# Merged batch rests, 512-token blocks, and float32 loads on SP's queue in a retention + feed-forward kernel

## The chip, the cores and the metric

The kernel runs on one core of a Trainium2 chip. The metric is the device time of one execution in microseconds (us); the median of three runs of the kernel before is 343.9 (343.79 to 344.42). The core has TensorE (PE in the profile; its weight loads are PEld), VectorE (DVE), ScalarE (ACT), GpSimd (POOL) and SyncE (SP). Here POOL and SP also issue DMA transfers: POOL those that change the type on the way, SP the others and the DMA transposes. SBUF is the working memory, PSUM the memory that TensorE writes its results to.

## The reference

Retention (attention without softmax, with a decay per head), then a feed-forward layer with hardswish:

```python
# q, k, v: (8 batches, 8 heads, 576 tokens, 64) float32
scores = scale * q @ k.T                      # scale = 1/8
gamma  = 1 - 2 ** (-5 - head)
ret    = scores * gamma ** (i - j)  where i >= j, else 0
x      = (ret @ v), heads side by side        # (4608, 512)
h      = x @ w_in                             # w_in  512 x 2048
g      = h * clip(h + 3, 0, 6) / 6
out    = g @ w_out                            # w_out 2048 x 512, out (4608, 512) float32
```

## The kernel before

**Retention, by chunks.** Each batch of 576 tokens is cut into four chunks of 128 tokens and a rest of 64, 40 chunks in all. The decay inside a chunk is split into factors: Q is multiplied by `gqk` (or `gqv[0]`), V by `gqv[1]`, so that only a 0/1 mask is left between them. What earlier chunks of the batch give to a chunk goes through a state, `ts`, which is kept in two block-diagonal tiles `tbd`, so that one matmul does two heads. A chunk takes these steps:

- load of q, k and v (L75): three transfers on POOL, float32 in DRAM to float16 in SBUF, runs of 64 elements;
- the transposes of Q and K to `qk`: chunks 0 to 5 by TensorE (L157, then VectorE L159/L163 or ScalarE L161), the others by DMA transposes on SP (L177), where Q is first scaled by VectorE together with V (`vs`, L181);
- `scores`: eight matmuls to PSUM `sc` (L192), then VectorE's multiplication with the mask to `at` (L196);
- `inter`: four matmuls of the state with Q (L208; left out in the first chunk of a batch);
- `intra_and_update`: eight matmuls of `at` with V, added to the same PSUM tile `o` (L218); eight matmuls for the update `u` (L227, not in the last chunk of a batch); ScalarE's copy of `o` to `xt16` (L230); VectorE's `ta` and `ts` (L234 to L238); ScalarE's two copies to `tbd` (L241, L242).

**Feed-forward, by blocks.** The 4608 rows of `xt16` are taken in nine blocks of 512, in the order of the tokens. A block spans chunks of two batches, as 512 does not divide by 576. `g1` (L258) makes one of 16 column groups of the hidden layer: four matmuls (L265) to a PSUM tile `ph`, of which there are three, ScalarE's relu to `u` (L269), VectorE's min and product to `gt` (L271). `g2` (L276) makes a quarter of the sum of one of the block's four output tiles: four matmuls (L283); after the fourth quarter ScalarE copies the tile (L287) and SP stores it (L289).

**The order** is written by hand: every engine works in the order of the program text. POOL issues chunks 0 to 3, the four parts of `win`, chunks 4 and 5, the four parts of `wout`, chunks 6 to 8 (L312 to L322), and later a chunk seven ahead of the one that is transposed (L372). Chunks 0 to 3 are done first; then g1 of block 0 begins with chunks 4 and 5 put between its units; then 192 columns of block 1. From there `run` (L387) puts the pieces of retention evenly between units of g1 of the next block and g2 of this one. `do_piece` (L369) is half a chunk's work: in its first half it issues chunk c's DMA transposes, in its second half it does `inter` of c−2, `scores` of c−1 and `intra_and_update` of c−2. VectorE's `at` and `vs` of the first chunks are put off by `later` until the unit after (`run_later`, L141).

Of the kernel before, what the change touches and what calls it, by code (L numbers as in the profile page):

```python
# [18 lines left out]
def kernel(  # L19
# [26 lines left out]
    NMB = NTOK // MBLK  # L46

    chunks = []
    for b in range(B):
        for s0 in range(0, S, P):  # L50
            chunks.append((b, s0, min(P, S - s0)))
    NCHK = len(chunks)
    lng = [float(np.log(1.0 - 2.0 ** (-5.0 - h))) for h in range(H)]

    const = ctx.enter_context(tc.tile_pool(name="const", bufs=1))
    big = ctx.enter_context(tc.tile_pool(name="big", bufs=1))
    nat = ctx.enter_context(tc.tile_pool(name="nat", bufs=10))
# [8 lines left out]
    loaded = {}  # L66

    def load_part(c, which):
        b, s0, n = chunks[c]
        if which == 0:  # L70
            loaded[c] = (nat.tile([P, 2, H, D], FP16, tag="qv", name=f"qv_{c}"),
                         nat.tile([P, H, D], FP16, tag="kn", name=f"kn_{c}"))
        qv, kn = loaded[c]
        t, src = ((qv[:, 0], q), (kn, k), (qv[:, 1], v))[which]
        nc.gpsimd.dma_start(t[0:n], src[b, :, s0:s0 + n, :].rearrange("h s d -> s h d"))  # L75

    def load_chunk(c):
        for which in range(3):
            load_part(c, which)

    def load_win(f0, f1):
        nc.gpsimd.dma_start(
            win16[:, :, f0:f1],
            moe_w_in.rearrange("(cc p) f -> p cc f", p=P)[:, :, f0:f1])

    def load_wout(c0, c1):
        nc.gpsimd.dma_start(
            wout16[:, c0:c1, :],
            moe_w_out.rearrange("(cc p) n -> p cc n", p=P)[:, c0:c1, :])


    load_part(0, 0)
# [8 lines left out]
    load_part(0, 1)  # L101
# [4 lines left out]
    load_part(0, 2)  # L106
# [14 lines left out]
    gc = const.tile([P, NPAIR], FP32)  # L121
    nc.scalar.activation(gc, lgc, ACTF.Exp, scale=float(P))
# [6 lines left out]
    for i in range(2):  # L129
        t = const.tile([P, NPAIR, P], FP16, name=f"tbd{i}")  # L130
        nc.vector.memset(t, 0.0)
        tbd.append(t)

    mask_b = mask01[:, None, :].to_broadcast([P, H, P])
    gc_b = gc[:, :, None].to_broadcast([P, NPAIR, D])


    st = {}
    later = []

# [4 lines left out]

    def transposes(c, apart=False):

        b, s0, n = chunks[c]
        qv, kn = loaded[c]
# [3 lines left out]
        ps = psum.tile([P, 2, NPAIR, P], FP16, tag="tu", name=f"tr_{c}")  # L153
        pk = psum.tile([P, NPAIR, P], FP16, tag="ph", bufs=3, name=f"trk_{c}") if apart else ps[:, 1]
        for dst, src in ((ps[:, 0], qv[:, 0]), (pk, kn)):
            for p in range(NPAIR):
                nc.tensor.transpose(dst[:, p, 0:n], src[0:n, 2 * p:2 * p + 2, :], ident16[0:n, 0:n])  # L157
        if apart:
            nc.vector.tensor_tensor(out=qk[:, 0, :, 0:n], in0=ps[:, 0, :, 0:n],  # L159
                                    in1=gqk[:, 0, :, 0:n], op=ALU.mult)  # L160
            nc.scalar.copy(qk[:, 1, :, 0:n], pk[:, :, 0:n])  # L161
        else:
            nc.vector.tensor_tensor(out=qk[:, :, :, 0:n], in0=ps[:, :, :, 0:n],  # L163
                                    in1=gqk[:, :, :, 0:n], op=ALU.mult)
        later.append(lambda: nc.vector.tensor_tensor(
            out=vs[0:n, 1], in0=qv[0:n, 1], in1=gqv[0:n, 1], op=ALU.mult))

    def transposes_by_dma(c):

        b, s0, n = chunks[c]  # L170
        qv, kn = loaded[c]
# [4 lines left out]
        def transpose(which, src):  # L176
            nc.sync.dma_start_transpose(qk[:, which, :, 0:n],  # L177
                                        src[0:n].rearrange("s h d -> s (h d)"))

        transpose(1, kn)  # L180
        nc.vector.tensor_tensor(out=vs[0:n], in0=qv[0:n], in1=gqv[0:n], op=ALU.mult)  # L181
        transpose(0, vs[:, 0])

    def scores(c):
        b, s0, n = chunks[c]
# [3 lines left out]
        for p in range(NPAIR):  # L189
            for h2 in range(2):  # L190
                r = slice(h2 * HALF, h2 * HALF + HALF)
                nc.tensor.matmul(sc[0:n, h2, p, 0:n], qk[r, 1, p, 0:n], qk[r, 0, p, 0:n],  # L192
                                 start=True, stop=True)
# [3 lines left out]
            out=at[0:n].rearrange("t a b s -> t (a b) s")[:, :, 0:n],  # L197
            in0=sc[0:n].rearrange("t a b s -> t (a b) s")[:, :, 0:n],
            in1=mask_b[0:n, :, 0:n], op=ALU.mult))

    def inter(c):
        b, s0, n = chunks[c]
        o = psum.tile([P, NPAIR, P], FP32, tag="o", name=f"o_{c}")
        st[c]["o"] = o
        if s0 == 0:
            return
        for p in range(NPAIR):
            nc.tensor.matmul(o[:, p, 0:n], tbd[c % 2][:, p, :], st[c]["qk"][:, 0, p, 0:n],  # L208
                             start=(p == 0), stop=False, skip_group_check=True)

    def intra_and_update(c):
        b, s0, n = chunks[c]
        qv, kn = loaded[c]
        o, at, vs = st[c]["o"], st[c]["at"], st[c]["vs"]
        for p in range(NPAIR):
            for h2 in range(2):
                r = slice(h2 * HALF, h2 * HALF + HALF)
                nc.tensor.matmul(o[r, p, 0:n], vs[0:n, 2 * p + h2, :], at[0:n, h2, p, 0:n],  # L218
                                 start=(s0 == 0 and p == 0), stop=(p == NPAIR - 1),
                                 skip_group_check=True)  # L220
        last = s0 + n == S
        if not last:
            u = psum.tile([P, NPAIR, D], FP32, tag="tu", name=f"u_{c}")
            for p in range(NPAIR):
                for h2 in range(2):
                    r = slice(h2 * HALF, h2 * HALF + HALF)
                    nc.tensor.matmul(u[r, p, :], kn[0:n, 2 * p + h2, :], vs[0:n, 2 * p + h2, :],  # L227
                                     start=(p == 0), stop=(p == NPAIR - 1), skip_group_check=True)
        g0 = b * S + s0
        nc.scalar.copy(xt16[:, :, g0:g0 + n], o[:, :, 0:n])  # L230
        if not last:
            ts = work.tile([P, NPAIR, D], FP16, tag="ts", bufs=2, name=f"ts_{c}")
            if s0 == 0:
                nc.vector.tensor_tensor(out=ts, in0=u, in1=gc_b, op=ALU.mult)  # L234
            else:
                ta = work.tile([P, NPAIR, D], FP32, tag="ta", bufs=2, name=f"ta_{c}")
                nc.vector.tensor_tensor(out=ta, in0=u, in1=st[c - 1]["ts"], op=ALU.add)  # L237
                nc.vector.tensor_tensor(out=ts, in0=ta, in1=gc_b, op=ALU.mult)  # L238
            st[c]["ts"] = ts
            nxt = tbd[(c + 1) % 2]  # L240
            nc.scalar.copy(nxt[0:HALF, :, 0:D], ts[0:HALF])  # L241
            nc.scalar.copy(nxt[HALF:P, :, D:2 * D], ts[HALF:P])  # L242
# [3 lines left out]
    def step(c, end=False):  # L246

        if c > 0:
            inter(c - 1)
        if not end:  # L250
            scores(c)
        if c > 0:
            intra_and_update(c - 1)


    gts = {}

    def g1(kb, fc, a, b_):  # L258
# [4 lines left out]
        ph = psum.tile([P, MBLK], FP32, tag="ph", bufs=3, name=f"ph_{kb}_{fc}_{a}")  # L263
        for dmc in range(NCC):
            nc.tensor.matmul(ph[:, 0:b_ - a], win16[:, dmc, P * fc:P * fc + P],  # L265
                             xt16[:, dmc, t0 + a:t0 + b_],
                             start=(dmc == 0), stop=(dmc == NCC - 1))
        u = work.tile([P, MBLK], FP32, tag="moeu", bufs=3, name=f"u_{kb}_{fc}_{a}")
        nc.scalar.activation(u[:, 0:b_ - a], ph[:, 0:b_ - a], ACTF.Relu,  # L269
                             bias=cb[:, 0:1], scale=1.0 / 6.0)  # L270
        nc.vector.scalar_tensor_tensor(out=gt[:, fc, a:b_], in0=u[:, 0:b_ - a], scalar=1.0,  # L271
                                       in1=ph[:, 0:b_ - a], op0=ALU.min, op1=ALU.mult)
# [3 lines left out]
    def g2(kb, mc, part, tag="pout"):  # L276
# [8 lines left out]
        if part == 3:  # L285
            osb = work.tile([P, DM], FP32, tag="osb", bufs=4, name=f"osb_{kb}_{mc}")
            nc.scalar.copy(osb, pout)  # L287
            r0 = kb * MBLK + P * mc
            nc.sync.dma_start(out[r0:r0 + P, :], osb)  # L289

    def g2_halves(kb, mc):
        gt = gts[kb]
        r0 = kb * MBLK + P * mc
        W = DM // 2
        for half in range(2):
# [7 lines left out]
            nc.sync.dma_start(out[r0:r0 + P, half * W:half * W + W], osb)  # L303


    def chunk_of(tok):
        b, s = divmod(tok, S)
        return b * ((S + P - 1) // P) + s // P

    WQ = DFF // 4  # L310
    NEAR = 9
    for c in range(1, 4):  # L312
        load_chunk(c)
    for i in range(4):
        load_win(i * WQ, i * WQ + WQ)
    for c in range(4, 6):
        load_chunk(c)
    for i in range(4):
        load_wout(4 * i, 4 * i + 4)
    for c in range(6, NEAR):  # L320
        load_chunk(c)
    next_load = [NEAR]  # L322


    transposes(0, apart=True)
    run_later(9)
    scores(0)
    run_later(9)
    for c in range(1, 4):
        transposes(c, apart=True)  # L330
        run_later(9)
        step(c)
        run_later(9)
    step(4, end=True)

    def unit1(kb, lo, hi, a=0, b_=MBLK):
        for fc in range(lo, hi):
            g1(kb, fc, a, b_)
            run_later(1)

    def start_of(c):
        b, s0, n = chunks[c]
        return b * S + s0


    unit1(0, 0, 9)
    make_gq()
    transposes(4)
    unit1(0, 9, 10)
    scores(4)  # L350
# [101 lines left out]
```

## Time and profile before

| what | value |
|---|---|
| median of 3 runs | 343.9 us |
| span of the profiled execution | 342.7 us |
| PE busy | 306.4 us (89%), 2304 matmuls |
| VectorE / ScalarE / GpSimd busy | 188.1 (55%) / 176.8 (52%) / 108.0 (32%) |
| loads issued by POOL (L75), q, k and v | 120, 0.86 to 0.88 us each at the mean |
| 512-column matmuls of g1 and g2 (mean) | 384 and 383 ns, overlapped |
| DMA packets on POOL's queue / on SP's | 116,736 / 38,736 |
| HBM read / written | 36.70 / 9.44 MB |

The profile is of one execution. A group line gives the line of the program, the engine, the operation, the output and its inputs, shapes and count, then the busy time, the mean duration, and the idle time ahead of it with what ended it. Timeline lines give the start and the length (from the first start to the last end when several instructions are merged, xcount), and in brackets the idle time before. Matmuls are pipelined, so their lengths overlap, and prices are better taken from start to start. The table of stages gives the busy time per engine in a stretch of the span.

### The profile page before, as it was taken

How to read it: one execution, taken by the hardware profiler on the slowest of the kernel's cores; microseconds unless marked ns; L12 is line 12 of the kernel's file. 1: busy time of each engine (PE TensorE's matmuls, PEld its weight loads, DVE VectorE, ACT ScalarE, POOL GpSimd, SP SyncE). 2: the span in 40 equal slices, each digit the busy share in tenths (PEclk: the TensorE clock that was granted, in tenths of full speed). 3: DMA queues.
4: the chain of work that ended last, by engine and by line, in shares of the span. 5: the costliest groups of instructions: out<-in, count | busy, mean ns of one | idle time of the engine just before them, and what ended most of it. 6: DMA issues, size and time to landing. Idle time of an engine off the chain costs nothing.

```text
span 342.7 us, 5990 instructions
## 1 busy us (share of the span) xinstructions
PE 306.4 (89%) x2304; PEld 158.1 (46%) x2304; DVE 188.1 (55%) x316; ACT 176.8 (52%) x327; POOL 108.0 (32%) x137
## 2 busy tenths in 40 slices
PE   2669767549989999999999999999999999999995
PEld 1443344225654454444455445444444444444444
DVE  2565675244676665666665766655576565443400
ACT  6346574034755565545555656545665556544411
POOL 8947389582338034603442344100000000000000
PEclk9999999896999999999999999999999999999999
DMA  9999999999699999977999499522133221000022
GB/s 62 148 202 183 193 141 150 159 154 175 84 123 149 125 100 145 146 94 90 111 129 133 81 135 142 83 70 63 48 78 76 65 71 37 31 33 31 31 80 76
DMA packets 155502, 36.19 MB, mean 106 GB/s; under 512 B 146641, under 2 KB 150993, under 8 KB 155473
## 3 DMA queue, kind: packets, MB, share of 16 engines
q0 software_dynamic: 116736, 18.36, 79.9%
q1 hardware_dynamic: 38736, 17.44, 23.5%
q8 instruction: 18, 0.29, 0.4%
q14 instruction: 12, 0.09, 0.1%
HBM read 36.70 MB, written 9.44 MB: 135 GB/s over the span
## 4 chain that ended last, share of the span: by engine, by line
PE 82%; DMA 5%; ACT 5%; DVE 3%; issue 2%; POOL 1%; SPq 0%; POOLq 0%; DVEq 0%; ACTq 0%
PE ph L265 36%; PE pout L283 34%; PE o L218 4%; DMA qk<-vs 4%; PE sc L192 4%; PE o L208 2%; ACT xt L230 2%; DVE gt L271 2%; ACT u L269 1%; DMA qv<-in_v_dram 1%; PE pout L298 1%; PE u L227 1%; DVE at L196 1%; POOL qv L75 1%; POOL kn L75 0%
## 5 line engine op out<-in xcount | busy, mean ns | idle before, releaser
L271 DVE SCALAR_TENSOR_TENSOR gt<-u,ph 128x512 f16<-128x512 f32 (+2 forms) x160 | 99.8, 631 | 91.8 <-ACT u L269 90.0
L265 PE MATMUL ph<-xt,win 128*128 128x512 f16 (+2 forms) x640 | 141.8, 365 | 6.5 <-ACT xt L230 4.8
L269 ACT ACTIVATE u<-ph,cb 128x512 f32<-128x512 f32 (+2 forms) x160 | 100.6, 644 | 67.2 <-PE ph L265 64.7
L283 PE MATMUL pout<-wout,gt 128*128 128x512 f16 x560 | 134.3, 383 | 0.0
L265 PEld LDWEIGHTS <-win 128*128 128x128 f16 x640 | 60.9, 99 | 68.7 <-issue 10.7
L283 PEld LDWEIGHTS <-gt 128*128 128x128 f16 x560 | 54.3, 98 | 63.8 <-issue 1.3
L75 POOL DMA_DIRECT2D kn<-in_k_dram x40 | 34.2, 856 | 98.8 <-PE u L227 80.9
L196 DVE TENSOR_TENSOR at<-sc,mask 128x1024 f16<-128x1024 f32 (+1 forms) x40 | 44.4, 1110 | 6.2 <-PE sc L192 6.2
L230 ACT CAST xt<-o 128x512 f16<-128x512 f32 (+1 forms) x40 | 21.7, 543 | 37.2 <-PE o L218 36.6
L287 ACT COPY osb<-pout 128x512 f32<-128x512 f32 x35 | 20.5, 585 | 35.6 <-PE pout L283 35.5
L75 POOL DMA_DIRECT2D qv<-in_q_dram x40 | 35.1, 877 | 3.1 <-DMA wout<-in_moe_w_out_dram 1.7
L75 POOL DMA_DIRECT2D qv<-in_v_dram x40 | 34.5, 862 | 4.0 <-DMA wout<-in_moe_w_out_dram 1.7
L192 PE MATMUL sc<-qk 64*128 64x128 f16 (+1 forms) x320 | 16.4, 226 | 13.0 <-DMA qk<-vs 9.2
L237 DVE TENSOR_TENSOR ta<-u,ts 128x256 f32<-128x256 f32 x24 | 10.1, 423 | 24.8 <-PE u L227 24.8
L181 DVE TENSOR_TENSOR vs<-qv,gqv 128x1024 f16<-128x1024 f16 (+1 forms) x34 | 23.0, 681 | 0.0
L241 ACT COPY tbd<-ts 64x256 f16<-64x256 f16 x32 | 12.9, 404 | 13.6 <-DVE ts L238 12.9
L192 PEld LDWEIGHTS <-qk 64*128 64x128 f16 (+1 forms) x320 | 9.7, 102 | 20.3 <-issue 13.1
L218 PE MATMUL o<-at,vs 128*64 128x128 f16 (+1 forms) x320 | 16.9, 231 | 1.8 <-DVE at L196 1.8
L208 PE MATMUL o<-qk,tbd 128*128 128x128 f16 (+1 forms) x128 | 12.4, 224 | 3.1 <-ACT tbd L242 3.1
L208 PEld LDWEIGHTS <-tbd 128*128 128x128 f16 x128 | 9.6, 103 | 11.3 <-ACT tbd L242 4.5
L218 PEld LDWEIGHTS <-vs 128*64 128x64 f16 (+1 forms) x320 | 10.4, 115 | 6.2 <-DVE at L196 2.3
L242 ACT COPY tbd<-ts 64x256 f16<-64x256 f16 x32 | 12.8, 401 | 0.4
(39 smaller groups left out, 72.7 us busy)
## 6 DMA issues: line engine op xcount, KB each, us to landing
out_dram<-osb SPq DMA_DIRECT2D x35, 256.0 KB, 2.4
qv<-in_q_dram POOLq DMA_DIRECT2D x32, 128.0 KB, 5.0
kn<-in_k_dram POOLq DMA_DIRECT2D x32, 128.0 KB, 4.5
qv<-in_v_dram POOLq DMA_DIRECT2D x32, 128.0 KB, 5.0
win<-in_moe_w_in_dram POOLq DMA_DIRECT2D x4, 512.0 KB, 10.4
wout<-in_moe_w_out_dram POOLq DMA_DIRECT2D x4, 512.0 KB, 9.5
qk<-kn SPq DMA_TRANSPOSE x34, 3.5
qk<-vs SPq DMA_TRANSPOSE x34, 2.6
```

Of the source, the lines that this page charges most:

```text
L75: nc.gpsimd.dma_start(t[0:n], src[b, :, s0:s0 + n, :].rearrange("h s d -> s h d"))
L181: nc.vector.tensor_tensor(out=vs[0:n], in0=qv[0:n], in1=gqv[0:n], op=ALU.mult)
L192: nc.tensor.matmul(sc[0:n, h2, p, 0:n], qk[r, 1, p, 0:n], qk[r, 0, p, 0:n], start=True, stop=True)
L196: later.append(lambda: nc.vector.tensor_tensor(out=at[0:n].rearrange("t a b s -> t (a b) s")[:, :, 0:n], in0=sc[0:n].rearrange("t a b s -> ...
L208: nc.tensor.matmul(o[:, p, 0:n], tbd[c % 2][:, p, :], st[c]["qk"][:, 0, p, 0:n], start=(p == 0), stop=False, skip_group_check=True)
L218: nc.tensor.matmul(o[r, p, 0:n], vs[0:n, 2 * p + h2, :], at[0:n, h2, p, 0:n], start=(s0 == 0 and p == 0), stop=(p == NPAIR - 1), skip_grou ...
L230: nc.scalar.copy(xt16[:, :, g0:g0 + n], o[:, :, 0:n])
L265: nc.tensor.matmul(ph[:, 0:b_ - a], win16[:, dmc, P * fc:P * fc + P], xt16[:, dmc, t0 + a:t0 + b_], start=(dmc == 0), stop=(dmc == NCC - 1))
L269: nc.scalar.activation(u[:, 0:b_ - a], ph[:, 0:b_ - a], ACTF.Relu, bias=cb[:, 0:1], scale=1.0 / 6.0)
L271: nc.vector.scalar_tensor_tensor(out=gt[:, fc, a:b_], in0=u[:, 0:b_ - a], scalar=1.0, in1=ph[:, 0:b_ - a], op0=ALU.min, op1=ALU.mult)
L283: nc.tensor.matmul(pout, gt[:, fc, P * mc:P * mc + P], wout16[:, fc, :], start=(fc == 0), stop=(fc == NFC - 1))
L287: nc.scalar.copy(osb, pout)
```

## The change

- **Pieces instead of chunks.** Each batch gives four pieces of 128 tokens. The rests of two batches are one piece of 128 rows: pieces 12, 21, 30 and 35 of 36. Such a piece has a block-diagonal mask, takes `inter` from two states, and makes no update. There are five `tbd` tiles that are handed out in turn. For odd batches the last state is scaled by the decay of 64 instead of 128 tokens.
- **Blocks of one batch.** `xt16` is ordered so that block kb, up to 7, is the first 512 tokens of batch kb, and block 8 holds all rests. The stores go to the matching rows; those of block 8 are two transfers of 64 rows each.
- **Loads.** Q and V are loaded as float32 by SP (`load_f32`), for the rests as two halves. VectorE casts V, and Q where it goes to a DMA transpose, in `vs`. For pieces 0 to 7 a GpSimd copy makes a float16 Q (`q16`). K of pieces 0 to 3 is loaded as float32 by SP too and cast by GpSimd; all other K stay on POOL as before. The float32 loads of pieces 4 to 7 wait for parts of win and wout to land. Later loads are issued four pieces ahead.
- **Start.** The transposes of pieces 0 to 7 are done by TensorE (before: chunks 0 to 5). In pieces 0 to 3, `update_mm` comes right after `scores`, and K is transposed before Q, each in its own PSUM tile.
- **Block 1** is done in four strips of 128 columns, each when its piece is ready; a `ph` tile then holds four column groups, so 16 matmuls of 128 columns take the place of four of 512.

The core of the diff:

```diff
-        t, src = ((qv[:, 0], q), (kn, k), (qv[:, 1], v))[which]
-        nc.gpsimd.dma_start(t[0:n], src[b, :, s0:s0 + n, :].rearrange("h s d -> s h d"))
+    def load_f32(dst, src, c, behind=None):
+        for p0, b, s0, n in pieces[c][3]:
+            dma = nc.sync.dma_start(dst[p0:p0 + n],
+                                    src[b, :, s0:s0 + n, :].rearrange("h s d -> s h d"))
...
+    def load_qv(c, behind=None):
+        qv = nat.tile([P, 2, H, D], FP32, tag="qv", bufs=6, name=f"qv_{c}")
+        loaded[c]["qv"] = qv
+        load_f32(qv[:, 0], q, c, behind)
+        load_f32(qv[:, 1], v, c)
...
+    def cast_early(c):
+        nc.gpsimd.tensor_copy(loaded[c]["kn"], loaded[c]["k32"])
+        q16 = nat.tile([P, H, D], FP16, tag="q16", bufs=3, name=f"q16_{c}")
+        loaded[c]["q16"] = q16
+        nc.gpsimd.tensor_copy(q16, loaded[c]["qv"][:, 0])
...
+        if kind == "main":
+            states = [(state_of[b], slice(0, P))]
+        else:
+            states = [(state_of[2 * b], slice(0, HALF)), (state_of[2 * b + 1], slice(HALF, P))]
+        for j, (state, cols) in enumerate(states):
+            for p in range(NPAIR):
+                nc.tensor.matmul(o[:, p, cols], tbd[state][:, p, :], qk[:, 0, p, cols],
+                                 start=(j == 0 and p == 0), stop=False, skip_group_check=True)
...
+        n = b_ - a
+        nf = MBLK // n
+        ph = psum.tile([P, nf, n], FP32, tag="ph", bufs=3, name=f"ph_{kb}_{f0}_{a}")
+        for j in range(nf):
+            for dmc in range(NCC):
+                fc = f0 + j
+                nc.tensor.matmul(ph[:, j, :], win16[:, dmc, P * fc:P * fc + P],
...
+    for c in range(EARLY):
+        cast_early(c)
+    wi = [load_win(i * WQ, i * WQ + WQ) for i in range(4)]
+    for c in (4, 5):
+        load_k16(c)
+        load_qv(c, behind=wi[c - 3])
+    wo = [load_wout(4 * i, 4 * i + 4) for i in range(4)]
+    for c in (6, 7):
+        load_k16(c)
+        load_qv(c, behind=wo[c - 4])
...
+    for c in range(EARLY):
+        transposes(c, apart=True)
+        run_later(9)
+        if c > 0:
+            inter(c - 1)
+            intra(c - 1)
+            update_state(c - 1)
+        scores(c)
+        update_mm(c)
+        run_later(9)
...
     def do_piece():
         c, half = divmod(done[0], 2)
         c += FIRST
-        while next_load[0] < NCHK and next_load[0] <= c + 7:
-            load_chunk(next_load[0])
-            next_load[0] += 1
+        load_until(c + 4)
...
+    run([unit1(0, f) for f in range(13)])
+    make_gq()
+    make_mask_rest()
+    first_half(4)
+    run([unit1(0, 13), unit1(0, 14)])
+    scores(4)
+    run([unit1(0, 15)])
+    first_half(5)
+    second_half(4)
+    scores(5)
+    run([unit1(1, f, 0, P) for f in (0, 4)])
+    second_half(5)
+    run([unit1(1, f, 0, P) for f in (8, 12)])
+    run([unit1(1, f, P, 2 * P) for f in range(0, NFC, 4)])
...
+    run([unit1(1, f, 2 * P, 3 * P) for f in range(0, NFC, 4)])
+    load_until(8)
+    first_half(7)
+    run([unit2(0, 3, 1)])
+    scores(7)
+    run([unit2(0, 3, 2)])
+    second_half(7)
+    run([unit2(0, 3, 3)])
+    gts.pop(0)
+    run([unit1(1, f, 3 * P, 4 * P) for f in range(0, NFC, 4)], 3)
+
+    run([unit2(1, mc, part) for mc in range(2) for part in range(4)], pieces_for(2))
```

`first_half(c)` is the GpSimd cast of Q and TensorE's transposes, `second_half(c)` is `inter`, `intra` and the update. From piece 8 on `do_piece` does what it did. The first `do_piece` falls into the last strip of block 1; its `load_until` issues pieces 9 to 12, and stands in SP's order behind the store of output tile (0, 3).

## The prediction

> **What bounds the kernel now.** I read the busy table, then the stages, then the chain of waits and the timelines inside the first two stages. The stage table (length, busy time of each engine, clock, DMA share, GB/s):
>
> ```profile
> core 0: us, PE busy (x) PEld busy (x) DVE busy (x) ACT busy (x) POOL busy (x), PEclk, DMA share, GB/s
> 0.00:24.36 24.36, 11.68 (x140) 8.44 (x141) 11.81 (x32) 11.66 (x28) 19.38 (x31) 1.00 1.44 133
> 24.36:78.55 54.19, 38.49 (x312) 20.70 (x312) 28.96 (x54) 25.22 (x55) 37.04 (x46) 0.95 2.14 167
> 78.55:339.30 260.75, 256.26 (x1852) 128.99 (x1851) 147.37 (x232) 139.67 (x244) 51.59 (x62) 0.99 0.78 91
> ```
>
> Three stages: **head** (0 to 24.36, until the first matmul of g1), **early** (to 78.55, where PE is idle 15.7 us) and **late** (PE busy 98%). Late can be shortened by less PE work only, head and early by removing waits. The early waits are seen in PE's timeline; the bracket is the idle time and what ended it:
>
> ```profile
> 62.96 0.61 PE L192 MATMUL sc<-qk 64*128 64x128 f16 x8 [4.75 <-DMA qk<-vs]
> ...
> 76.88 0.42 PE L192 MATMUL sc<-qk 64*64 64x64 f16 x8 [3.52 <-DMA qk<-vs]
> ```
>
> So TensorE waits for DMA transposes of chunks 6 to 9, in a time in which POOL issues loads back to back. Unit prices come from start-to-start distances in the same timeline, where PE is never idle:
>
> ```profile
> 37.34 0.39 PE L157 MATMUL tr<-ident,qv 128*128 128x128 f16 x4
> 37.57 0.39 PE L157 MATMUL tr<-ident,kn 128*128 128x128 f16 x4
> 37.79 1.03 PE L265 MATMUL ph<-xt,win 128*128 128x512 f16 x4
> ...
> 126.82 0.39 PE L208 MATMUL o<-qk,tbd 128*128 128x128 f16 x4
> 127.14 0.40 PE L192 MATMUL sc<-qk 64*128 64x128 f16 x8
> 127.47 0.41 PE L218 MATMUL o<-at,vs 128*64 128x128 f16 x8
> 127.71 0.29 PE L227 MATMUL u<-vs,kn 128*64 128x64 f16 x8
> 127.94 1.90 PE L283 MATMUL pout<-wout,gt 128*128 128x512 f16 x8
> ```
>
> Four 128-column matmuls take 0.23 us (transposes) to 0.32 us (inter). A full chunk costs 0.32 + 0.33 + 0.24 + 0.23 = 1.12 us. Eight 512-column matmuls take 1.73 us in the chain of waits, so g1 or g2 of a block is 64 of them, 13.84 us. A half chunk costs 0.69 us (0.21 at 84.75, 0.24 at 108.00, 0.24 at 85.29).
>
> **Late stage.** Of its 264.15 us to the end of the span I count 252.9 as PE work: columns 192 to 511 of block 1 in g1 (8 matmuls per 1.10 us at 85.53: 8.8), half of g2(0) (6.9), seven g1 (96.9), eight g2 (110.7), the chunks 9 to 39 (24 × 1.12 − 6 × 0.32 for the first of a batch + 7 × 0.69 − 0.24 done before = 29.6). The other 11.2 us are the tail (3.4), the wait for xt at each block (0.55) and small waits. After the change this stage begins with g1(2): half of g2(1) 6.9, seven g1 96.9, seven g2 96.9, and pieces 12 to 35: twenty full ones (22.4 − 5 × 0.32) and four merged rests. A merged rest costs 8 × 0.0525 (inter, 64 columns) + 0.33 + 0.24 = 0.99 us against 2 × 0.69; scores of piece 12 come earlier. Sum 24.4, total 225.1. I keep the 11.2 us of waits and add 0.5, since the last block's rows go out in two stores each (an SP issue of 0.33 and a little): **236.8 us**.
>
> VectorE's vs now reads float32. The nearest rows are the f16 one of before and the one with a float32 input from PSUM of the same size:
>
> ```profile
> L196 DVE TENSOR_TENSOR at<-sc,mask 128x1024 f16<-128x1024 f32 x32 | 39.0, 1218 | 6.2 <-PE sc L192 6.2
> L181 DVE TENSOR_TENSOR vs<-qv,gqv 128x1024 f16<-128x1024 f16 x27 | 18.3, 683 | 0.0
> ```
>
> I take the first, 1.22 us, so 28 × 0.54 = 15 us more on VectorE. It is 57% busy in the late stage and becomes about 62%, so I cost that at nothing there; its cover is ph's three buffers. If it is gone, each of 24 pieces costs up to 0.54 us, 13 us. Loads now run four pieces ahead instead of seven; at about 7 us a piece that is 28 us, against a median of 5.0 from issue to landing, so nothing is charged for it.
>
> **Head.** Before, `at` of chunks 0 to 3 starts at 8.57, 13.53, 17.59 and 21.50, and g1 2.86 us after the last. After, SP starts the loads at about 1.2 us with no constants between them, but two GpSimd casts per piece are new. No cast is in the trace: iota of 64 and 128 elements took 0.20 and 0.26, which extends to 0.61 us for 512; affine_select of 128 took 0.30, four times that is 1.2. I take 0.8, nearer the lower row, since both only write or copy. The first load landed 3.46 us after its issue (4.78 − 1.32); a 256 KB store on SP took 2.4. Between, the first K is there at about 4.1, the first cast Q near 6, the first `at` near 8.0. Then VectorE sets the pace in the new order: qk 0.42, vs 0.68, ta 0.42, ts 0.42, at 1.22 = 3.17, with gaps 3.25 us per piece against 4.3 on average before. The last `at` starts at 17.75, and 2.65 later (tbd is ready sooner) g1 starts: **20.4 us**; bounds 19.5 (casts 0.61) and 24.4 (nothing gained). Loads hold this while three take under 3.25 us. The win loads now queue behind the casts on POOL, about 14.5 instead of 13.12, but behind fewer open loads; they landed 2.5 us apart before, so the first lands near 20. A late one costs its delay one to one. Three more memsets of tbd (0.27 each) and one more exp (0.19) lie in the first 4 us, where both engines wait for loads; uncovered they cost 1.0.
>
> **Early.** Work from the first g1 to g1(2): g1(0) 13.84; g1 of block 1 in four strips, 16 groups of 16 matmuls at 4 × 0.23, 14.7 (20.5 by the inter row; I take the transposes, which like these run many in a row); g2(0) 13.84; half of g2(1) 6.92; pieces 4 to 7 with transposes 4 × 1.58 − 0.32 = 6.0; pieces 8 to 11 and the scores of 12, 4.5. Sum 59.8. Waits that stay: the slow start of the clock (36 matmuls took 10.05 instead of 7.8) 2.3; `at` and qk of pieces 4 and 5, as now 1.3 + 1.8 and some, 4.3; pieces 6 and 7, 1.
>
> The new wait is on **SP**. In the program's order the loads of pieces 9 to 12 stand behind the store of (0, 3), and the DMA transposes of piece 8 behind these ten loads. The issue time of a float32 load of 1,024 runs on SP, I, is not in the trace. The rows (SPq, start, duration):
>
> ```profile
> 60.96 0.64 SPq L289 DMA_DIRECT2D out_dram<-osb  x1
> 61.71 1.29 SPq L177 DMA_TRANSPOSE qk<-kn  x1
> ...
> 73.55 0.33 SPq L289 DMA_DIRECT2D out_dram<-osb  x1
> ```
>
> Bounds: 0.33 (a store alone) and 1.29 (a transpose); POOL took 0.87 for the same 1,024 runs. I take **0.6**, the row of the same kind of instruction on the same queue with another in front. From the end of g2(0) on PE: store issued 1.85 us later; six loads and four halves at 0.75 I, 9 I; two transposes 2.5; landing 1.4 after the last issue; then four more pieces, each 2 I + 2.5, one store 0.5, and 1.1 from the scores of piece 12 to g1(2). That is 17.35 + 17 I = **27.5 us**, in which PE has 3.7 + 6.9 + 4.5 = 15.1 of work: 12.4 of wait, the place of the 15.7 now. Early: 59.8 + 2.3 + 4.3 + 1 + 12.4 = **79.8**.
>
> **Sum.** 20.4 + 79.8 + 236.8 = 337.0 us of span. The median of the runs, 343.9, stands 1.2 over the profiled span of 342.7; with that **338.2 us**, −1.7%. About 4 of the 5.7 us are the head's; the strips and rests give the rest.
>
> The Trainium skill, "DMA: Bandwidth & Descriptors", section Issuing engines are not separate DMA queues, says that loads issued from another engine run on the same DMA engines and save only issue time. By it the head could gain at most 12 × (0.87 − 0.6) = 3.2 us from the queue, and the sum would be 339.0; POOL's 0.87 per load in the trace neither proves nor denies it, as landing and issue keep the same pace. "SBUF — State Buffer", section SBUF: two separate sides, says that a VectorE instruction with two SBUF inputs and a GpSimd one that reads SBUF shut each other out. By it four vs of 0.68 would delay the head's casts by up to 2.7 us, an estimate, and the sum would be 340.9. The trace has no GpSimd cast beside a vs; a load issue beside one did not stretch (0.95 at 11.38, against 0.94 and 0.95 around it).
>
> **Rivals.**
> 1. *SP becomes the bound* (slower). If a load holds SP as a transpose does, 1.2 us, the early stretch is 37.8 instead of 27.5 and the head's twelve loads cost 1.8 more: 349.1 of span, 350.3 us. It decides from I = 0.6 + 5.7/17 = 0.93 us on. For it: eight times as many runs as a store, and transposes that copy short runs take 1.2. Against it: the issue of both stores differs by what stands in front, not by size.
> 2. *The head is held by its chain anyway*: casts and first landing eat what the order saves, g1 starts near 24 and the new SP wait replaces the old: 341 of span, 342.3 us.
> 3. *It is better than I think*: with I = 0.33 the 27.5 become 23.0, 333.7 us, and with g1 at 19.5 it is 332.8.
> 4. *VectorE binds late*: 338.2 + up to 13 us, 345 to 351.
>
> **Chances.** Forecast (335 to 341) 0.47, rival 1 (345 to 352) 0.25, rival 2 (341 to 344) 0.10, rival 3 (330 to 335) 0.13, rival 4 0.05. One measurement can tell 0.2%, 0.7 us, from no change. Faster: 0.47 + 0.13 + 0.06 of rival 2 = 0.66; same 0.04; slower 0.30. The range 331 to 351 takes in both bounds of I.
>
> **What would show it.** The issue row of the float32 loads on SP (0.6); first g1 matmul near 20.4; the casts' rows (0.8); vs at 1.22; groups of 16 strip matmuls every 0.92 us; PE's wait for piece 8's scores near 6.7 us with the ten loads in front on SP; late stage 237 us. I am wrong if I exceeds 0.93, if POOL's late casts hold piece 4, or if the late stage shows waits for gt.

## The result and the profile after

The changed kernel takes **362.2 us** (median of 4 runs, 360.9 to 364.9) against 344.2 for the kernel before on the same chip: ratio 1.052, interval 1.050 to 1.055. The forecast of 338.2 was wrong in sign, and the time lies above the range. The profiled execution took 364.9 us, 2.7 more than the median, so spans of it are a little long.

The table of stages of the kernel after, cut at the first matmul of g1 and at the first of g1(2), as the prediction was:

```profile
core 0: us, PE busy (x) PEld busy (x) DVE busy (x) ACT busy (x) POOL busy (x), PEclk, DMA share, GB/s
0.00:22.46 22.46, 12.25 (x140) 8.25 (x141) 13.18 (x34) 11.65 (x29) 11.65 (x24) 1.00 1.01 170
22.46:118.96 96.50, 71.62 (x672) 43.81 (x673) 48.96 (x71) 37.36 (x70) 17.73 (x24) 0.88 1.15 158
118.96:363.20 244.24, 228.60 (x1572) 112.24 (x1571) 139.64 (x194) 124.09 (x209) 15.26 (x19) 0.98 0.69 108
```

Predicted were 20.4, 79.8 and 236.8. All three are longer, the early stage by 16.7 us, and there the granted clock is 0.88. The late stage too has lost 7.4 us. PE's timeline shows where the early stage stands still:

```profile
43.39 0.40 PE L219 MATMUL tr<-ident,q 128*128 128x128 f16 x4 [2.61 <-POOL q L204]
...
45.17 3.52 PE L343 MATMUL ph<-xt,win 128*128 128x128 f16 x32
...
51.89 0.64 PE L282 MATMUL o<-at,vs 128*64 128x128 f16 x8 [2.98 <-DVE at L252]
...
97.34 0.61 PE L248 MATMUL sc<-qk 64*128 64x128 f16 x8 [11.07 <-DMA qk<-vs]
```

The waits that matter most lie in two places: around piece 5 at 43 to 52 (its transposes, then its product with V), and the scores of piece 8 at 97, whose wait was predicted at 6.7 and is 11.07. One more, of 3.93 us at 113.70, comes behind the second. The line at 45.17 is one to note: 32 strip matmuls in 3.36 us to the next start, where 16 take 0.89 us elsewhere. SP's queue ahead of the second place:

```profile
83.36 0.37 SPq L94 DMA_DIRECT2D qv<-in_q_dram  x1
83.78 0.69 SPq L94 DMA_DIRECT2D qv<-in_v_dram  x1
84.58 1.27 SPq L94 DMA_DIRECT2D qv<-in_q_dram  x1
85.90 1.21 SPq L94 DMA_DIRECT2D qv<-in_v_dram  x1
87.22 0.85 SPq L94 DMA_DIRECT2D qv<-in_q_dram  x1
88.12 1.12 SPq L94 DMA_DIRECT2D qv<-in_v_dram  x1
89.35 1.86 SPq L94 DMA_DIRECT2D qv<-in_q_dram  x2
91.25 1.30 SPq L94 DMA_DIRECT2D qv<-in_v_dram  x2
92.67 1.29 SPq L235 DMA_TRANSPOSE qk<-kn  x1
94.06 1.20 SPq L235 DMA_TRANSPOSE qk<-vs  x1
```

The ten loads of pieces 9 to 12 hold SP from 83.36 to 92.55, and the transposes of piece 8 come behind them, as foreseen. What was not foreseen is the price. The first load takes 0.37 us, and from the third on most take 0.85 to 1.3. The issue becomes slow when loads are already open. By m1, below, it is not the instruction that costs this but the pace of the data.

What else the prediction named (VectorE's and POOL's groups; the cast of Q is the last line):

```profile
L238 DVE TENSOR_TENSOR vs<-qv,gqv 128x1024 f16<-128x1024 f32 x28 | 34.1, 1218 | 1.3 <-DMA qv<-in_v_dram 1.3
```

```profile
L204 POOL CAST q<-qv 128x512 f16<-128x512 f32 x4 | 2.5, 616 | 20.8 <-DMA qv<-in_q_dram 11.5 <-PE o L282 9.3
```

### The profile page after: what moved, and what is told of

Its sections match the earlier page's. It is cut to its first block, busy times and chain, and to the rows that moved or that the text cites. A ratio compares the mean times of both kernels' runs of the same rounds, so it can differ in the third digit from the quotient of the medians.

```text
span 363.2 us, 6067 instructions
## 1 busy us (share of the span) xinstructions
PE 312.5 (86%) x2384; PEld 164.3 (45%) x2384; DVE 201.8 (56%) x299; ACT 173.1 (48%) x308; POOL 44.6 (12%) x65
## 4 chain that ended last, share of the span: by engine, by line
PE 65%; DMA 15%; SPq 6%; DVE 6%; ACT 3%; issue 3%; POOL 1%; DVEq 0%; ACTq 0%
PE pout L370 30%; PE ph L343 27%; DMA qv<-in_v_dram 5%; DMA qk<-vs 5%; SPq L94 5%; PE o L282 3%; PE sc L248 3%; DMA win<-in_moe_w_in_dram 2%; DVE gt L349 2%; DVE at L252 2%; DMA qv<-in_q_dram 1%; DVE vs L238 1%; PE o L270 1%; ACT xt L286 1%; PE pout L383 1%
## 5 line engine op out<-in xcount | busy, mean ns | idle before, releaser
L343 PE MATMUL ph<-xt,win 128*128 128x512 f16 (+1 forms) x768 | 142.6, 338 | 6.0 <-ACT xt L286 4.0
L349 DVE SCALAR_TENSOR_TENSOR gt<-u,ph 128x512 f16<-128x512 f32 x144 | 97.2, 685 | 87.0 <-ACT u L348 86.5
L348 ACT ACTIVATE u<-ph,cb 128x512 f32<-128x512 f32 x144 | 97.4, 687 | 62.8 <-PE ph L343 59.9
L286 ACT CAST xt<-o 128x512 f16<-128x512 f32 x36 | 21.1, 586 | 58.4 <-PE o L282 58.2
L252 DVE TENSOR_TENSOR at<-sc,mask 128x1024 f16<-128x1024 f32 x32 | 39.0, 1219 | 12.6 <-PE sc L248 12.5
L248 PE MATMUL sc<-qk 64*128 64x128 f16 x288 | 16.0, 237 | 24.6 <-DMA qk<-vs 22.9
L238 DVE TENSOR_TENSOR vs<-qv,gqv 128x1024 f16<-128x1024 f32 x28 | 34.1, 1218 | 1.3 <-DMA qv<-in_v_dram 1.3
L319 ACT COPY tbd<-ts 64x256 f16<-64x256 f16 x32 | 12.9, 404 | 19.4 <-DVE ts L312 16.9
L282 PE MATMUL o<-at,vs 128*64 128x128 f16 x288 | 16.7, 244 | 3.2 <-DVE at L252 3.0
L311 DVE TENSOR_TENSOR ta<-u,ts 128x256 f32<-128x256 f32 x24 | 10.1, 423 | 16.6 <-PE u L297 16.5
L282 PEld LDWEIGHTS <-vs 128*64 128x64 f16 x288 | 10.6, 120 | 7.5 <-issue 3.0
L297 PE MATMUL u<-vs,kn 128*64 128x64 f16 x256 | 10.4, 206 | 0.8 <-DVE qk L224 0.4
```

The source lines that it names most:

```text
L238: nc.vector.tensor_tensor(out=vs, in0=qv, in1=gqv, op=ALU.mult)
L248: nc.tensor.matmul(sc[:, h2, p, :], qk[r, 1, p, :], qk[r, 0, p, :], start=True, stop=True)
L252: later.append(lambda: nc.vector.tensor_tensor(out=at.rearrange("t a b s -> t (a b) s"), in0=sc.rearrange("t a b s -> t (a b) s"), in1=mas ...
L282: nc.tensor.matmul(o[r, p, :], vs[:, 2 * p + h2, :], at[:, h2, p, :], start=(st[c]["first"] and p == 0), stop=(p == NPAIR - 1), skip_group ...
L286: nc.scalar.copy(xt16[:, :, g0:g0 + P], o)
L343: nc.tensor.matmul(ph[:, j, :], win16[:, dmc, P * fc:P * fc + P], xt16[:, dmc, t0 + a:t0 + b_], start=(j == 0 and dmc == 0), stop=(j == nf ...
```

## The experiments

**Theories.** A: float32 loads cost about 1.2 us each, and those of pieces 9 to 12 hold the DMA transposes back on SP. B: Q and V of piece 5 crawl beside the wout loads. C: the merged rests, 512-token blocks and strips cost the time themselves. A has two readings: 256 KB written as float32 costs this on any queue (A1), or SP's queue does (A2). D came after e3: what the merged rests and blocks gain is given back in waits for DMA transposes, since five pieces' transposes stand between the store of (0, 3) and g1(2). The runs come from several chips, each with its own runs of the kernel before; the ratios are to those, and across chips they are what to compare (the medians before lie between 343.9 and 344.7 us, so a difference of two runs in us can be off by some 0.7).

| run | us | ratio to before, interval |
|---|---|---|
| after | 362.2 | 1.052 (1.050 to 1.055) |
| e1 loads early | 355.7 | 1.032 (1.027 to 1.037) |
| e2 wout later | 365.5 | 1.063 (1.056 to 1.069) |
| e3 loads by POOL | 345.9 | 1.004 (1.001 to 1.007) |
| e5 piece 5 first | 355.7 | 1.032 (1.029 to 1.035) |
| e6 both orders | 351.9 | 1.021 (1.017 to 1.025) |
| e7 TensorE to piece 11 | 336.7 | 0.978 (0.975 to 0.981) |
| e8 transposes sooner | 342.8 | 0.989 (0.982 to 0.996) |
| e9 TensorE to piece 12 | 337.8 | 0.980 (0.975 to 0.985) |
| e10 float32, TensorE to 11 | 341.1 | 0.990 (0.987 to 0.993) |
| e12 before, TensorE to chunk 9 | 340.8 | 0.990 (0.986 to 0.993) |
| e13 transposes one ahead | 332.7 | 0.967 (0.961 to 0.972) |

The profiled executions by stretch, all from starts in PE's timeline: head to the first g1; then to the start of block 1's last strip; then to the first g1(2); then late. "Waits" is the idle time in brackets behind the start of the first g1, up to that of the first g1(2); "clock" is the granted clock of the two middle stretches together.

| run | head | to strip | to g1(2) | late | waits | clock |
|---|---|---|---|---|---|---|
| predicted | 20.4 | 52.3 | 27.5 | 236.8 | | |
| after | 22.5 | 58.8 | 37.7 | 244.2 | 24.3 | 0.88 |
| e1 | 22.4 | 60.0 | 31.8 | 240.3 | 20.1 | 0.90 |
| e5 | 22.4 | 54.2 | 38.6 | 238.8 | 25.0 | 0.89 |
| e6 | 22.6 | 54.2 | 31.4 | 242.0 | 17.5 | 0.92 |
| e3 | 21.0 | 53.3 | 28.5 | 240.5 | 16.8 | 0.96 |
| e10 | 22.4 | 55.4 | 24.9 | 236.8 | 12.9 | 0.95 |
| e7 | 20.8 | 55.0 | 23.8 | 236.8 | 11.5 | 0.93 |
| e13 | 20.7 | 53.3 | 20.6 | 235.9 | 10.1 | 1.00 |

**e1: the loads of pieces 8 to 11 ahead of g2(0).**

```diff
+    load_until(11)
     order = [(0, 0), (0, 1), (1, 0), (1, 1), (0, 2), (1, 2), (0, 3), (1, 3)]
...
-    load_until(8)
     first_half(7)
```

> The changed kernel, with the loads of pieces 8 to 11 issued ahead of the stores of block 0 (before the first g2) instead of behind them. Theory A (the loads of pieces 9 to 12 start only behind the store of (0, 3), and each takes 1.2 us on SP's queue, with the DMA transposes of piece 8 behind them): eight of the ten loads in front of piece 8's transposes are gone, TensorE's wait of 11.1 us for them falls to about 3, the later waits shrink too, 362 becomes 349 to 355 us. Theory C (merged rests and strips are what costs): within 2 us of 362.

The stretch to g1(2) fell from 37.7 to 31.8 and the wait for the scores of piece 8 from 11.07 to 3.86; the waits at piece 5 stayed (2.57 and 3.40). So the position of the loads is worth 6.6 us of the loss; the 355.7 lies just outside the expected 349 to 355.

**e2: wout behind V of piece 5.**

```diff
     wo = [load_wout(4 * i, 4 * i + 4) for i in range(4)]
+    after(wo[0], last_v[0])
```

> The changed kernel, with the first wout load waiting until V of piece 5 has landed. Theory B (Q and V of piece 5 crawl beside the wout loads, about 155 packets per us each, so that the cast of Q and the mask of piece 5 are late): TensorE's waits of 2.6 and 3.0 us at pieces 4 and 5 go, 362 becomes 355 to 358 us; g2(0) still finds wout landed. Theories A and C: those two waits are not the larger part, at most these 5.6 us go and the 11.1 us before piece 8 stay.

Slower, which neither theory had. POOL works in order: the wout issue that now waited (16.44 us, to 38.15) stood ahead of the cast of Q of piece 4, which came at 42.83, and PE waited 6.47 us for it. So the time tells nothing of B, though the waits at pieces 4 and 5 behind this one are 2.19 and 1.58 us, as later in e5, which repeats the edit without the late cast.

**e3: Q, K and V as float16 by POOL; pieces, blocks and strips kept.** Loads run seven pieces ahead, as before the change, with ten buffers; there are no casts, and the loads of pieces 1 to 3 stand behind the constants on POOL.

```diff
-            dma = nc.sync.dma_start(dst[p0:p0 + n],
+            dma = nc.gpsimd.dma_start(dst[p0:p0 + n],
...
-        qv = nat.tile([P, 2, H, D], FP32, tag="qv", bufs=6, name=f"qv_{c}")
+        qv = nat.tile([P, 2, H, D], FP16, tag="qv", bufs=10, name=f"qv_{c}")
...
-        load_until(c + 4)
+        load_until(c + 7)
```

> The changed kernel with one part undone: Q, K and V are loaded as float16 by POOL as in the kernel before, there are no GpSimd casts, loads run seven pieces ahead again, ten buffers; merged rests, 512-token blocks and strips stay. Theories A and B (SP's float32 loads are the cost): the waits for DMA transposes fall to those of before, g1 starts near 23.5 and the late stage lasts 237, in sum 338 to 347 us. Theory C: stays above 355.

16.3 us of the 18 went, so C is out as the cause of the loss: it is the loads, with what e3 undid along with them (the casts, the lead of four pieces). But the rest of the change gains nothing either. Its waits for DMA transposes (in total, how many, the longest), the second line, are like those of before, the first, in another place:

```profile
PE sc L192 <- DMA qk<-vs: 9.2, 3, 4.7
```

```profile
PE sc L235 <- DMA qk<-vs: 11.0, 3, 4.8
```

**m1: the loads alone.** It computes nothing and fills the output with zeros. Twelve loads each: a, SP as float32; b, POOL as float16; c, POOL as float32; then d (SP, float32) and e (POOL, float16) together; then f (SP, float32) beside four wout loads. Each phase starts when the one before has landed.

> Loads alone, nothing is computed and the output is filled with zeros: phases of twelve loads of 128 x 8 x 64: float32 by SP; float16 by POOL; float32 by POOL; then SP float32 and POOL float16 together; then SP float32 beside four wout loads by POOL. Theory A1 (writing 256-byte packets is what costs, whatever the queue): SP 1.2 us per load, POOL float16 0.9, POOL float32 1.2. Rival A2 (it is SP's queue): POOL float32 0.9. Together: if the DMA engines are the limit, a pair takes 2.0 to 2.1 us; if the queues have limits of their own, 1.2. Beside wout: both queues move equal numbers of packets, about 150 per us, so a float32 load takes 6 to 7 us while wout lasts.

The timeline (start, length from first to last issue):

```profile
0.74 12.59 SPq L51 DMA_DIRECT2D a<-in_q_dram  x12
...
17.27 10.65 POOL L51 DMA_DIRECT2D b<-in_k_dram  x12 [16.83 <-DMA a<-in_q_dram]
31.63 10.54 POOL L51 DMA_DIRECT2D c<-in_v_dram  x12 [3.71 <-DMA b<-in_k_dram]
48.68 24.21 SPq L51 DMA_DIRECT2D d<-in_q_dram  x12
...
78.68 24.79 SPq L51 DMA_DIRECT2D f<-in_v_dram  x12
...
106.69 23.73 SPq L87 DMA_DIRECT2D out_dram<-z  x36
```

From start to start, a takes 16.5 us, b 14.4 and c 17.0. POOL issues c as fast as b, but c's data lands as late as a's: the float32 width sets the pace, not SP's queue (A1). The packet records give 850 packets of 256 bytes per us for a, 1.20 us per load; for b, in its steady part, 1,084 per us, 0.94 us per load, so POOL's 0.87 to 0.89 is its issue and not the pace of the data. c moves in packets of 4,096 bytes, 53.7 per us, 1.19 us per load: the pace of a. d and e together take 30.0 us, 2.5 us a pair where 2.0 to 2.1 were expected, and about a and b in sum (30.9): the two queues move data as one set of DMA engines would, and using both at once gains nothing. f's twelve issues take 24.79 instead of 12.59 us; while wout loads, each queue moves some 152 packets per us, so a load of 1,024 packets gets 6.7 us. wout's packets carry a whole row of 512 elements, so packet for packet the short runs lose.

**e5: piece 5 ahead of wout, with the casts moved too.**

```diff
+    cast_q(4)
+    cast_q(5)
     wo = [load_wout(4 * i, 4 * i + 4) for i in range(4)]
+    after(wo[0], last_v[0])
...
-        cast_q(c)
+        if c > 5:
+            cast_q(c)
```

> The kernel after, with the GpSimd casts of Q of pieces 4 and 5 placed ahead of the four wout loads on POOL, and the first wout load waiting for V of piece 5. Nothing else moves. Theory B (the float32 loads of piece 5 crawl beside wout, because both queues get the same number of packets) expects them to land about 4 us after issue instead of 19, PE's waits of 2.61 and 2.98 us at piece 5 to shrink to the 2.2 and 1.6 us of the kernel with POOL loads, the first matmul of g2(0) to come some 4 us earlier than 59.3, and 357 to 359 us. Theory A alone (all the loss is at the loads of pieces 9 to 12) expects 361 to 363 us and the same waits under other names. A loss by wout itself would show as a wait for wout at the first g2(0), and the time would stay at 362 or rise. The wait of 11 us at the scores of piece 8 stays in all cases.

B holds, and is larger than expected: 6.6 us, and the first g2(0) comes at 54.51 instead of 59.28. The loads of piece 5 land 8.3 to 8.8 us after their issue (about 4 were expected), and the waits for `at` of pieces 4 and 5 are 2.19 and 1.58 us, as expected. wout, issued from 38.36 us instead of 21.79, holds nothing. In the kernel after, the chain of work that ended last shows the load that crawled:

```profile
27.48 2.36 SPq L94
29.89 19.50 DMA qv<-in_v_dram
```

**e6: both orders.** The edits of e1 and e5 together.

> The two order changes together: loads of pieces 8 to 11 ahead of g2(0), and piece 5 ahead of wout. If the two losses are separate places, the gains add: 355.7 for the first alone, less 3 to 5, makes 350 to 353 us. If DMA time as a whole is the bound up to piece 12 (float32 loads of 1.20 us each), bringing piece 5 forward only moves the wait to pieces 8 to 11, and the time stays at 354 to 356 us. In no case does it reach the 346 of the loads by POOL, if the price of a float32 load is real.

10.3 us of the 18: more than either, less than the sum of 13.2. What is left to e3, 6.9 us of span, lies in every stretch: 1.6 in the head, then 0.9, 2.9 and 1.5.

**e7: e3, and pieces 8 to 11 transposed by TensorE.**

```diff
-            if c < NP:
+            if c < 12:
+                first_half(c)
+            elif c < NP:
                 transposes_by_dma(c)
```

> Loads by POOL as float16, merged rests, blocks and strips kept, and pieces 8 to 11 transposed by TensorE instead of by DMA. In the kernel with loads by POOL, PE waits three times, 11.0 us together, for the DMA transposes of pieces 8 to 11. Theory D (what the merged rests and blocks gain is given back because five pieces' transposes of 2.5 us each on SP must fit between the store of (0,3) and g1(2)) expects these waits to go, for 4 x 0.46 us more of TensorE and some new waits of 1 to 2 us for VectorE: 345.9 - 11.0 + 1.8 + 1.5 = 338 us, 336 to 341. The rival (loads themselves come too late, or VectorE is what the pieces wait for) expects waits of the same size for loads or VectorE: 344 to 347 us.

D's step for pieces 8 to 11 holds; this is the first version faster than before, by 2.2%.

**e8: e3, with the DMA transposes of pieces 8 and 9 issued during g2(0).**

```diff
+    load_until(8)
+    transposes_by_dma(8)
     run([unit2(0, 2, 0), unit2(0, 2, 1)])
...
+    load_until(9)
+    transposes_by_dma(9)
     first_half(7)
```

> Loads by POOL as float16; the DMA transposes of pieces 8 and 9 issued during g2(0), ahead of the stores of (0,2) and (0,3) on SP, with six buffers for qk and vs instead of four. Theory D expects the waits at pieces 8 and 9 (3.16 and most of 4.80) to go, the one of 3.02 to stay or shrink: 338 to 341 us. If the DMA transposes are slowed by loads in flight, so that early issue only stretches them (they took 1.2 to 2.2 us there), 342 to 346 us.

Missed: 342.8, ratio 0.989 against 1.004, in the range of the rival, which had the transposes stretched by loads in flight. The trace doesn't show that: their median from issue to landing is 4.9 us for K and 3.6 for Q, against 4.7 and 3.2 in e3. The wait at piece 8 went, but 5.02 and 3.22 us came back at later pieces (94.63 and 108.06): two pieces with a lead don't give the next ones one. The diff leaves out the larger buffers (six of qk and vs).

**e9: e7, with piece 12 too by TensorE** (`c < 13`).

> As the kernel with POOL loads and TensorE transposes to piece 11 (336.7 us), with piece 12, the first merged rest, transposed by TensorE too. There, the scores of piece 12 wait 3.47 us for DMA transposes ahead of g1(2). Theory D expects this wait to go for 0.46 us of TensorE: 333.5 to 335.5 us. If VectorE or the copies to tbd take its place, 336 to 338.

Missed: the wait went from piece 12 to piece 13, and grew:

```profile
104.45 0.61 PE L235 MATMUL sc<-qk 64*128 64x128 f16 x8 [4.26 <-DMA qk<-vs]
```

Its transposes had been issued at 94.77 and 96.17, and the three of this stretch took 7.2 to 8.5 us to land. In e7 (3.47 us at piece 12) and here, the first piece that goes by DMA waits.

**e10: e6 with pieces 8 to 11 by TensorE**, their Q cast by GpSimd; the edit of e7 on e6.

> Float32 loads on SP, both order changes (351.9 us), and pieces 8 to 11 transposed by TensorE, their Q cast by GpSimd. It differs from the kernel with TensorE transposes to piece 11 and POOL loads (336.7) in the loads and casts. If the price of the float32 loads is only felt through the transposes behind them on SP, the waits of 3.90, 1.11 and 4.17 us go for 1.84 of TensorE: 343 to 346 us, or near 338 if the later waits (3.70 and 1.72) go with them. If the loads as data are late by themselves, PE waits for the casts of Q of pieces 8 to 11 instead: 348 to 353.

341.1, below the expected 343 to 346, as the later waits went with the earlier ones (one of 4.20 at piece 12 stays). With the orders mended and TensorE on the transposes, float32 loads on SP, with their casts and the lead of four pieces, cost about 4 us against e7 (ratio 0.990 against 0.978), 1.6 of them in the head.

**e12: the kernel before, with chunks 6 to 9 by TensorE.**

```diff
-            if c < NCHK:
+            if c < 10:
+                transposes(c)
+            elif c < NCHK:
                 transposes_by_dma(c)
```

> The kernel before, with chunks 6 to 9 transposed by TensorE and nothing else. It tells whether the merged rests, blocks and strips have a worth of their own, or whether the gain of the kernel with POOL loads comes from the transposes alone. Its waits for DMA transposes are 9.2 us together, 8.3 of them in the early stage. If they go for 4 x 0.46 us less the half chunk, 344.2 - 8.3 + 1.6 + 1.0 = 338 to 340 us, and the merged rests, blocks and strips would be worth the 2 us or so to 336.7. If the loads of chunks 6 to 9 are what is late, 342 to 345, and the merging is worth more.

340.8 lies between the two ranges expected: 1.0% faster than before, where e7 is 2.2%. So pieces, blocks, strips and the new start are worth about 1.2%, 4 us, once the transposes don't hold them. Here too the first chunk that goes by DMA waits, 4.93 us.

**e13: e7, with each DMA transpose issued one piece sooner**, and six buffers of qk and vs.

```diff
-            elif c < NP:
-                transposes_by_dma(c)
+            if 12 <= c + 1 < NP:
+                transposes_by_dma(c + 1)
```

> As the kernel with POOL loads and TensorE transposes to piece 11 (336.7 us), with the DMA transposes of every later piece issued one piece sooner, and six buffers for qk and vs. When piece 12 too was transposed by TensorE, the wait did not go but moved to piece 13 (4.26 us), whose transposes took 7 to 8 us from issue to landing. If that latency, against one piece of lead, is the whole wait, a second piece of lead takes it away: 336.7 - 3.5 = 333 us, 332 to 335. If the transposes wait behind a store or for VectorE's vs, the wait moves again and the time stays at 336 to 338.

332.7 us, 3.3% faster than before and the fastest of all. PE's waits for DMA transposes:

```profile
PE sc L235 <- DMA qk<-vs: 0.7, 1, 0.7
```

Their time from issue to landing did not fall (median 5.1 us for K and 3.3 for Q, against 4.2 and 2.9 in e7), and six buffers without a lead for every piece had left 9.9 us of such waits (e8). So the wait was latency against too short a lead, and not the transposes' throughput.

## Why the prediction was wrong

**The failed step** is the price of a float32 load. The prediction took SP's issue of it, I, as 0.6 us, between a store (0.33) and a transpose (1.29), and charged nothing for its data. Alone, an issue does take 0.37 to 0.58. But back to back the data sets the pace, 1.20 us (m1). The ten loads took 9.2 us; with the prediction's 9 I that is I = 1.02, over the 0.93 it had named as the point where its sign turns. The row to ask was not one of SP's issues: it was how fast the DMA engines move 256-byte runs. POOL's 0.87 for the same runs as float16 was in the profile, but as an issue time, and it is no bound on the pace of float32 data.

- **Early, to g1(2).** 37.7 us instead of 27.5. Rival 1, with I = 1.2, had 37.8: mechanism and place were right, at a chance of 0.25. That the size came out is partly luck: the ten loads took 9.2 us and not 10.8, the eight after piece 8's transposes 4.3 and not 9.6, and what made up for it were the eight transposes of pieces 9 to 12, 13.2 us instead of 10, and 2.3 us in which SP issued nothing. It still gave 350.3, since the next three points were in no case.
- **Early, piece 5.** 58.8 instead of 52.3 to the last strip. The prediction kept 4.3 us of waits for pieces 4 and 5 and did not ask what the loads of piece 5 run beside. e5 brought this to 54.2: 4.6 us are the wout loads'.
- **The clock.** The prediction counted waits at their length. In the kernel after, the clock is about half behind them:

```profile
core 0: us, PE busy (x) PEld busy (x) DVE busy (x) ACT busy (x) POOL busy (x), PEclk, DMA share, GB/s
...
45.17:48.70 3.53, 3.53 (x38) 3.53 (x36) 0.18 (x1) 1.49 (x3) 0.00 (x0) 0.53 1.45 185
...
59.28:66.00 6.72, 6.72 (x35) 3.07 (x33) 1.38 (x2) 1.16 (x2) 1.04 (x2) 1.00 1.04 66
...
97.34:102.70 5.36, 5.36 (x40) 2.44 (x39) 2.35 (x2) 0.07 (x1) 0.00 (x0) 0.50 0.96 186
```

The stretches shortly behind the waits of 2.61 and 11.07 us run at 0.53 and 0.50; g2(0), behind steady work, runs at 1.00. In the early stage, 96.5 − 24.3 of waits leaves 72.2 us of work; in e13 the same work takes 73.9 − 10.1 − 1.8 (the added transposes) = 62.0. The difference, 10.2 us, is what the slow clock and waits too short to be listed cost. 7.8 us of it stand in the trace: in four stretches at 0.50 (45.06 to 48.47, 51.89 to 55.30, 89.44 to 103.09, 113.33 to 116.74) TensorE was busy for 15.6 us, twice what the work takes at 1.00. The 2.3 predicted were for the slow start of g1 alone, and there 52 matmuls took 14.23 us, 3.0 more than at 0.216 each (1.73 for eight). e5 shows the clock's part best: its listed waits are no shorter (25.0 us), yet its early stage is 3.8 us shorter, as TensorE's busy time in it falls from 71.62 to 67.40 us. The Trainium skill, "TensorE: Matmul & The Clock Gate", section What's actually happening, says that the clock halves after an idle window of about 3.4 us and comes back after about as long of steady work. The 0.50 behind 11.07 us of wait agrees, though it lasted for 5.36 us of steady work and not 3.4; ahead of the 0.53 there were only 3.05 us of idle in 4.8, in two pieces.

- **Late.** 244.2 instead of 236.8: waits for DMA transposes went on (5.50 us at 129.17, 1.72 at 154.98), and all listed waits behind the start of g1(2) are 11.5 us against 4.0 in e13. The lead of four pieces, for which the prediction charged nothing, is not the cause: e10 keeps it, and its late stage is 236.8 us, as that of e7 with a lead of seven. e10 differs from e6 (242.0) only in the transposes of pieces 8 to 11, so the lateness was carried over from there. The sum for the stage was right (236.8 in e7 and e10, 235.9 in e13), and VectorE did not bind (rival 4): e10 has `vs` from float32, e7 from float16.
- **Head.** 22.46 instead of 20.4. The condition was stated, that three loads take under 3.25 us; at 1.20 each they take 3.6, and the four `at` (8.01 to 19.50) start 3.8 us apart at the mean. 0.80 us is g1's wait for the first part of win. With POOL's loads and no casts it is 20.8 (e7), near the forecast.
- **Right in size.** vs of float32 1.218 (1.22 taken); strips 0.89 per 16 matmuls (0.92); casts 0.616, the lower bound (0.8 taken).
- **The gain that was meant.** Even with the loads undone (e3) the change gave nothing. The merged rest puts pieces 8 to 12 between the store of (0, 3) and g1(2), and their DMA transposes come too late there. The prediction saw this wait and kept most of it (12.4 us in the place of 15.7); it did not ask what it would be worth to remove it, some 13 us (e3 against e13).

The Trainium skill, "DMA: Bandwidth & Descriptors", section Specifications, gives 512 bytes as the least size of a transfer for the full rate. m1 agrees in direction: 218 GB/s for a, which reads runs of 256 bytes, 381 GB/s for stores of 2 KB rows. The prediction did not weigh the rule; but the runs read are 256 bytes in both kernels, so it does not by itself tell them apart, as m1's 1.20 us for a and 0.94 for b do.

What stays open: how the 4 us between e7 and e10 divide between load pace, casts and a lead of four pieces instead of seven, and how far the DMA transposes' latency (3.0 us at the median of the kernel after for qk<-vs, 7 to 8 us in e9 between POOL's loads) is due to loads in the same engines. Neither was tried alone. Why the same runs move slower when they are written as float32 no run shows.

## What to carry to other kernels

When loads move to another queue, price the data and not the issue: ask what the shared DMA engines move per us at that run length and width, and what else is in flight, since a queue of short runs gets its share by packets and not by bytes. Before a load is placed on a queue, name what stands behind it there, and give DMA transposes a lead as long as their latency under load. And a wait of some us on TensorE is to be charged with the slow clock behind it.

## What the runs showed of the hardware

- The same 256-byte reads moved at 1.20 us per 128 x 512 load when written as float32 and at 0.94 when POOL's transfer cast them to float16 (16.5 and 14.4 us for twelve, from start to start); POOL writing float32 was as slow as SP (17.0 us).
- SP's issue of a load grew from 0.37 to 1.3 us with loads open in its queue: a long issue can be a sign of data that is behind.
- A queue beside wout's loads: 152 packets per us each, a 256 KB load in 6.7 us instead of 1.20.
- An instruction that waits for a DMA blocks all behind it on its engine, also where the engine is idle: POOL's wout issue in e2, 16.44 us, with a cast behind it.
- TensorE's half clock came in stretches of 3.41 us and of four times that (13.65) in the early stage of the kernel after, so that a wait of 3 us in two pieces cost a whole stretch.
